# Holding back eight of the sixteen layer-2 pieces behind units 4 and 5, so that twelve are in store at each border between chunks

## The chip, the cores and the metric

The kernel runs on one core of a Trainium2 chip. The core has five engines that each take their own instructions in order: TensorE (PE in the profile; its weight loads are shown as PEld), VectorE (DVE), ScalarE (ACT), GpSimd (POOL) and SyncE (SP). SP does no arithmetic here; it only issues DMA transfers, one after the other. The metric is the time of one execution on the device in microseconds.

## The reference

Two stages follow each other. The first is a linear attention with a decaying state, for 4 batch entries, 8 heads, 768 steps and a head width of 48:

```python
for t in range(S):
    cur = np.einsum('bhd,bhe->bhde', u[None] * kt, vt)
    y[:, :, t] = np.einsum('bhd,bhde->bhe', rt, state + cur)
    state = w[None, :, :, None] * state + np.einsum('bhd,bhe->bhde', kt, vt)
```

Its output, laid out as 3072 tokens of 384 numbers, goes through a two-layer MLP with 2048 hidden units: `h = x @ w_in`, `g = h * sigmoid(h)`, `out = g @ w_out`.

## The kernel before

The 768 steps are cut into 6 chunks of 128 steps. A unit is one chunk of one batch entry, so there are 24 units, and units 4c to 4c+3 make up chunk c. For one unit the attention work is:

- `load` (line 74): three DMA transfers on SP's queue bring r, k and v.
- `turn` (line 204): TensorE transposes r and k into PSUM, and `decay` (line 210) multiplies both by their decay factors on VectorE.
- `product_pair` (line 237): for two units together, TensorE multiplies the decayed k with the decayed r. It reads the results of both `decay` calls.
- `masked` (line 244): VectorE masks the product.
- `outputs` (lines 260, 265, 275): TensorE makes the attention output (tile `yp`) and the state's increment (tile `sp`).
- `evict_y` (line 288): VectorE adds the bonus and writes `y`.
- `turn_y` (line 319): for units 6 and up a DMA transpose on SP's queue puts `y` into `xT`, the input of the MLP. For the units before, TensorE does it.
- `state` (line 299): VectorE adds the increment to the state. GpSimd makes the products with u, the decayed k and the bonus (lines 165, 167, 171, 181).

The MLP of a chunk is cut into pieces. `first(sc)` has sixteen layer-1 pieces, each of three matmuls of 128x512 (line 335) with a SiLU on ScalarE (line 338). They read `xT` of all four units of the chunk. `second(sc)` has sixteen layer-2 pieces, each of four matmuls of 128x384 (line 347); four such pieces make one block of 128 tokens, which ScalarE copies out of PSUM (line 352) and SP's queue stores (line 356).

The pieces stand in a list, `fillers`, and `fill(n)` writes the next n of them into the program at that place. If the list has run out, it writes nothing. The order of the instructions on each engine is the order in which the Python code calls them. The main loop goes over pairs of units, 4 and 5, then 6 and 7, and so on to 22 and 23. In each pass there are six places where pieces go in: four behind the product, two between the outputs of the two units, two behind the outputs, two and two around the casts of r for the next pair (`cast_r`), and four at the end. That is sixteen in one pass. With the second pair of a chunk all of `xT` has been asked for, and the chunk's 32 pieces are added to the list, just behind `outputs(i + 1)`. This place is called a border here. There are five: with units 7, 11, 15, 19 and 23.

The list begins with four layer-1 pieces and the sixteen layer-2 pieces of chunk 0. The pass of units 4 and 5 takes sixteen of these twenty. At the borders, in the kernel before, the list is empty when the 32 new pieces come.

Of the kernel before, what the change touches and what calls it, by code (L numbers as in the profile page):

```python
# [15 lines left out]
def kernel(  # L16
# [13 lines left out]
    B, H, S, D = r.shape  # L30
# [19 lines left out]
    def unit(i):  # L50
        return divmod(i, B)
# [26 lines left out]
    def load(i):  # L78
        if i >= NU:
            return  # L80
        ld(i, rin, r)
        ld(i, kin, k)
        ld(i, vin, v)
# [75 lines left out]
    def L(i):  # L159
        return live.setdefault(i, {})  # L160

    def bonus_products(i):
        n = i % NIN
        ku = wrk.tile([128, H, D], FP, name="ku")
        nc.gpsimd.tensor_tensor(out=ku, in0=kin[n][:, :, 0:D], in1=u_bc, op=ALU.mult)  # L165
        L(i)["rku_f"] = wrk.tile([128, H, D], FP, name="rku_f")
        nc.gpsimd.tensor_tensor(out=L(i)["rku_f"], in0=rin[n][:, :, 0:D], in1=ku, op=ALU.mult)  # L167

    def decayed_k(i):
        eng = nc.vector if i < B else nc.gpsimd  # L170
        eng.tensor_tensor(out=kc[i % NIN][:, :, 0:D], in0=kin[i % NIN][:, :, 0:D],  # L171
                                in1=lamC, op=ALU.mult)
# [23 lines left out]
    def turn(i):  # L196
        n = i % NIN
        t = L(i)["t"] = next_att().rearrange("p y (x g t) -> p y x g t", x=2, g=NP)
        for x, src in enumerate((rin, kin)):
            flat = src[n].rearrange("p h d -> p (h d)")  # L200
            for p in range(NP):
                for y in range(2):
                    rows = slice(HC * y, HC * y + HC)
                    nc.tensor.transpose(t[0:PR, y, x, p, :], flat[rows, 128 * p:128 * p + PR],  # L204
                                        ident[rows, rows])

    def decay(i):
        for x, key, lam in ((0, "rT", lamR), (1, "kT", lamK)):
            L(i)[key] = wrk.tile([PR, NP, C], FP, name=key)
            nc.vector.tensor_tensor(  # L210
                out=L(i)[key].rearrange("p g (y t) -> p y g t", y=2),
                in0=L(i)["t"][0:PR, :, x], in1=lam.rearrange("p g (y t) -> p y g t", y=2),
                op=ALU.mult)
# [13 lines left out]
    def product_pair(i):  # L227
        a = [next_att().rearrange("p j (g c) -> p j g c", g=NP) for _ in range(2)]
        for e in range(2):
            L(i + e)["a"] = a[e]  # L230
        for s0, c0 in ((0, 0), (HC, HC)):
            for p in range(NP):
                for e in range(2):
                    rT, kT = L(i + e)["rT"], L(i + e)["kT"]
                    o0 = s0 if e == 0 else HC - s0
                    for j, r0 in ((0, 0), (1, 64)):
                        nc.tensor.matmul(a[e][o0:o0 + HC, j, p, c0:C],  # L237
                                         kT[r0:r0 + D, p, s0:s0 + HC],
                                         rT[r0:r0 + D, p, c0:C],
                                         start=True, stop=True)  # L240

    def masked(i):
        am = L(i)["am"] = wrk.tile([128, 2, NP, C], F16, name="am")
        nc.vector.tensor_tensor(  # L244
            out=am.rearrange("p h g c -> p (h g) c"), in0=L(i)["a"].rearrange("p h g c -> p (h g) c"),
            in1=(maskX if crossed(i) else maskM).unsqueeze(1).broadcast_to([128, H, C]), op=ALU.mult)

    def outputs(i):
        sc, b = unit(i)
        v16, vy = L(i)["v16"], L(i)["vy"]  # L250
        if sc:
            yp = ps.tile([128, 512], FP, name="yp", tag="moe", bufs=4)
            L(i)["y"] = yp[:, 0:HD]
        else:
            ys = next_att()
            L(i)["y"], L(i)["sps"] = ys[:, 0, 0:HD], ys[:, 1, 0:HD]
        y = L(i)["y"].rearrange("p (h d) -> p h d", h=H)
        for p in range(NP):
            if sc:
                nc.tensor.matmul(y[:, 2 * p:2 * p + 2, :],  # L260
                                 L(i)["rT16"][0:PR, p, :],
                                 st16[b][:, p, :], start=True, stop=False)
            for j in range(2):
                h = 2 * p + j
                nc.tensor.matmul(y[:, h, :], L(i)["am"][:, j, p, :], vy[:, h, :],  # L265
                                 start=not sc, stop=(not sc or j == 1))
        if sc < NCH - 1:
            if sc:
                sp = ps.tile([128, 512], FP, name="sp", tag="moe", bufs=4)
                L(i)["sps"] = sp[:, 0:HD]  # L270
            sps = L(i)["sps"].rearrange("p (g n) -> p g n", g=NP)
            kf = kc[i % NIN].rearrange("p h d -> p (h d)")
            vf = v16.rearrange("p h d -> p (h d)")
            for p in range(NP):
                nc.tensor.matmul(sps[:, p, :], kf[:, 128 * p:128 * p + 128],
                                 vf[:, PW * p:PW * p + PW], start=True, stop=True)

    def decayed_state(i):
        sc, b = unit(i)
        if 0 < sc < NCH - 1:  # L280
            L(i)["sdec"] = wrk.tile([PR, NP, PW], FP, name="sdec")
            nc.gpsimd.tensor_tensor(out=L(i)["sdec"], in0=st[b],  # L282
                                    in1=wCT.unsqueeze(2).broadcast_to([PR, NP, PW]), op=ALU.mult)

    def evict_y(i):
        y = L(i)["y"].rearrange("p (h d) -> p h d", h=H)
        L(i)["y16"] = wrk.tile([128, H, D], F16, name="y16")
        nc.vector.tensor_tensor(out=L(i)["y16"], in0=y, in1=L(i)["vu"], op=ALU.add)  # L288

    def state(i):  # L290
        sc, b = unit(i)
        if sc == NCH - 1:
            return
        sps = L(i)["sps"].rearrange("p (g n) -> p g n", g=NP)
        for p0, c0 in ((0, 0), (64, D)):
            dst = st[b][p0:p0 + D, :, c0:c0 + D]
            src = sps[p0:p0 + D, :, c0:c0 + D]
            if sc:
                nc.vector.tensor_tensor(out=dst, in0=src,  # L299
                                        in1=L(i)["sdec"][p0:p0 + D, :, c0:c0 + D], op=ALU.add)  # L300
            else:
                nc.scalar.copy(out=st16[b][p0:p0 + D, :, c0:c0 + D], in_=src)
                nc.scalar.copy(out=dst, in_=src)
        if sc:
            nc.gpsimd.tensor_copy(out=st16[b], in_=st[b])
# [8 lines left out]
    def turn_y(i, by_pe):  # L314
        sc, b = unit(i)
        yf = L(i)["y16"].rearrange("p h d -> p (h d)")
        x = x_tile(sc)
        if not by_pe:
            nc.sync.dma_start_transpose(out=x[:, :, b, :], in_=yf)
            return  # L320
        yT = ps.tile([128, NQ, C], F16, name="yT", tag="moe", bufs=4)
        for q in range(NQ):
            nc.tensor.transpose(yT[:, q, :], yf[:, 128 * q:128 * q + 128], ident16)  # L323
        nc.scalar.copy(out=x[:, :, b, :], in_=yT)  # L324
# [35 lines left out]
    def fill(n):  # L360
        for _ in range(n):
            if fillers:
                fillers.pop(0)()

    def second(sc):
        return [lambda b=b, p=p: l2(sc, b, p) for b in range(B) for p in range(4)]

    def first(sc):
        return [lambda f=f: l1(sc, 0, B, f) for f in range(NFT)]
# [99 lines left out]
    for i in range(B, NU, 2):  # L469
        sc, b = unit(i)  # L470
        nxt = range(i + 2, min(i + 4, NU))
        product_pair(i)
        for n in nxt:
            bonus_products(n)
            decayed_k(n)
        masked(i)
        masked(i + 1)
        fill(4)
        outputs(i)
        evict_y(i)  # L480
        turn_y(i, i < 6)
        state(i)
        fill(2)
        outputs(i + 1)
        evict_y(i + 1)
        turn_y(i + 1, i < 6)
        state(i + 1)
        if b:
            fillers.extend(first(sc) + second(sc))
        fill(2)  # L490
        for n in nxt:
            turn(n)
            decay(n)
        load(i + NIN)
        load(i + 1 + NIN)
        for n in nxt:
            bonus_sum(n)
            cast_v(n)
            bonus_v(n)
            decayed_state(n)  # L500
        for n in nxt:
            fill(2)
            cast_r(n)
        fill(4)
    fill(len(fillers))


# [28 lines left out]
```

## Time and profile before

| | |
|---|---|
| median of 3 runs | 224.25 us (222.26 to 226.5) |
| the profiled execution | 223.16 us |
| its span, first to last instruction | 221.5 us |
| TensorE busy | 187.8 us, 85% of the span |
| GpSimd, ScalarE, VectorE busy | 117.4, 106.5, 101.7 us |
| mean granted clock of TensorE | 0.974 |

The profile lists, for each engine, what ran when, how long the engine had been idle ahead of it, and what ended the idle time. The granted clock is 1.00 at 2.4 GHz and 0.50 at 1.2 GHz; a value between them is a stretch that had both.

### The profile page before, as it was taken

The page shows a single profiled execution, that of the slowest core. Times are in us where ns is not written, and L with a number is a line of the kernel's source. Part 1 is how long each engine was busy: PE and PEld are TensorE (multiplying, and loading weights), DVE is VectorE, ACT ScalarE, POOL GpSimd, SP SyncE. Part 2 cuts the span into 40 slices and gives each one's busy share as a digit, 9 for nine tenths or more (in the row PEclk, how much of TensorE's full clock was granted, in tenths as well). Part 3 has the DMA queues.
Part 4 walks back from the last instruction along what each step waited for, and adds up shares of the span by engine and source line. Part 5 has one row for each costly group of instructions (what it writes and reads, how often), then busy time and mean ns, then how long its engine had stood idle before and what let it go on. Part 6 is the DMA issues. An engine that isn't in the chain of part 4 may idle for free.

```text
span 221.5 us, 5379 instructions
## 1 busy us (share of the span) xinstructions
PE 187.8 (85%) x2178; PEld 119.9 (54%) x2178; DVE 101.7 (46%) x175; ACT 106.5 (48%) x212; POOL 117.4 (53%) x151
## 2 busy tenths in 40 slices
PE   2566897989939999949999949999949999679993
PEld 1445576856715566725566615566724666424561
DVE  4675475646446266536463626464626553400021
ACT  4402758937108783019763119663129761138500
POOL 8676549995951964942956912956914902000000
PEclk9999999999996999999999988999999999979998
DMA  6899999915848017748029266019276012210011
GB/s 122 176 194 192 225 187 178 210 22 123 200 113 174 3 21 150 188 111 175 4 41 236 90 152 127 3 36 226 98 162 127 0 39 74 78 30 0 3 71 71
DMA packets 90265, 24.54 MB, mean 111 GB/s; under 512 B 83328, under 2 KB 90240, under 8 KB 90240
## 3 DMA queue, kind: packets, MB, share of 16 engines
q1 hardware_dynamic: 85824, 20.65, 42.7%
q0 software_dynamic: 3712, 3.15, 9.2%
q10 hardware_dynamic: 704, 0.40, 0.9%
q8 instruction: 17, 0.28, 0.5%
q14 instruction: 8, 0.07, 0.1%
HBM read 20.84 MB, written 4.72 MB: 115 GB/s over the span
## 4 chain that ended last, share of the span: by engine, by line
PE 72%; issue 7%; DVE 6%; DMA 5%; POOL 5%; ACT 2%; SPq 1%; ACTq 0%; POOLq 0%; DVEq 0%
PE hps L335 31%; PE ops L347 23%; PE att L237 6%; PE att L204 6%; DMA xT<-y 3%; PE att L224 2%; DMA u_bc<-in_u_dram 2%; DVE st L299 2%; DVE y L288 1%; POOL rku_f L167 1%; POOL ku L165 1%; PE yp L265 1%; PE yp L260 1%; PE yT L323 1%; ACT xT L324 1%
## 5 line engine op out<-in xcount | busy, mean ns | idle before, releaser
L335 PE MATMUL hps<-xT,win 128*128 128x512 f16 (+1 forms) x336 | 71.5, 368 | 18.0 <-DMA xT<-y 10.5
L338 ACT ACTIVATE gT<-hps 128x512 f16<-128x512 f32 x96 | 54.8, 603 | 36.2 <-PE hps L335 34.3
L347 PE MATMUL ops<-wout,gT 128*128 128x384 f16 x384 | 65.9, 326 | 0.0
L335 PEld LDWEIGHTS <-win 128*128 128x128 f16 x336 | 32.9, 103 | 47.9 <-issue 18.6
L181 POOL TENSOR_TENSOR vu<-vin,rku 128x384 f32<-128x384 f32 x24 | 19.8, 829 | 55.0 <-DVE rku L176 55.0
L347 PEld LDWEIGHTS <-gT 128*128 128x128 f16 x384 | 36.2, 98 | 23.0
L244 DVE TENSOR_TENSOR am<-att,maskM 128x1024 f16<-128x1024 f32 x14 | 17.1, 1223 | 37.9 <-PE att L237 35.4
L352 ACT COPY osb<-ops 128x384 f32<-128x384 f32 x20 | 9.6, 478 | 44.0 <-PE ops L347 44.0
L210 DVE TENSOR_TENSOR rT<-att,lamR 112x512 f32<-112x512 f32 x24 | 16.5, 686 | 30.3 <-PE att L204 15.0
L167 POOL TENSOR_TENSOR rku_f<-rin,ku 128x384 f32<-128x384 f32 x24 | 24.7, 1028 | 1.9
L165 POOL TENSOR_TENSOR ku<-kin,u_bc 128x384 f32<-128x384 f32 x24 | 24.1, 1005 | 2.8 <-DMA u_bc<-in_u_dram 1.9
L171 POOL TENSOR_TENSOR kc<-kin,lamC 128x384 f16<-128x384 f32 x20 | 20.0, 1000 | 0.0
L288 DVE TENSOR_TENSOR y<-yp,vu 128x384 f16<-128x384 f32 x20 | 11.1, 557 | 15.7 <-PE yp L265 5.1
L204 PE MATMUL att<-ident,rin 64*112 64x64 f32 x192 | 12.0, 255 | 5.8 <-DMA rin<-in_r_dram 4.0
L210 DVE TENSOR_TENSOR kT<-att,lamK 112x512 f32<-112x512 f32 x24 | 16.3, 679 | 0.0
L237 PEld LDWEIGHTS att<-rT,kT 48*64 48x64 f32 x640 | 14.3, 133 | 3.5 <-issue 3.5
L237 PE MATMUL att<-rT,kT 48*64 48x64 f32 (+1 forms) x640 | 15.7, 247 | 0.0
L204 PEld LDWEIGHTS att<-ident,rin 64*112 64x112 f32 x192 | 8.8, 155 | 11.1 <-issue 4.5
L176 DVE TENSOR_REDUCE rku<-rku_f 128x8 f32<-128x384 f32 x24 | 12.3, 541 | 4.0 <-POOL rku_f L167 4.0
L282 POOL TENSOR_TENSOR sdec<-st,wCT 112x384 f32<-112x384 f32 x16 | 13.2, 827 | 0.0
L354 DVE COPY osb<-ops 128x384 f32<-128x384 f32 x4 | 2.2, 557 | 23.7 <-PE ops L347 23.7
L244 DVE TENSOR_TENSOR am<-att,maskX 128x1024 f16<-128x1024 f32 x10 | 12.1, 1214 | 0.0
(57 smaller groups left out, 176.2 us busy)
## 6 DMA issues: line engine op xcount, KB each, us to landing
rin<-in_r_dram SPq DMA_DIRECT2D x24, 192.0 KB, 3.6
kin<-in_k_dram SPq DMA_DIRECT2D x24, 192.0 KB, 3.8
vin<-in_v_dram SPq DMA_DIRECT2D x24, 192.0 KB, 3.7
out_dram<-osb SPq DMA_DIRECT2D x24, 192.0 KB, 2.4
win<-in_moe_w_in_dram POOLq DMA_DIRECT2D x4, 384.0 KB, 6.0
wout<-in_moe_w_out_dram POOLq DMA_DIRECT2D x4, 384.0 KB, 8.2
xT<-y SPq DMA_TRANSPOSE x18, 2.3
u_bc<-in_u_dram ACTq DMA_DIRECT2D x1, 192.0 KB, 5.1
```

What stands on the lines that cost most here:

```text
L165: nc.gpsimd.tensor_tensor(out=ku, in0=kin[n][:, :, 0:D], in1=u_bc, op=ALU.mult)
L167: nc.gpsimd.tensor_tensor(out=L(i)["rku_f"], in0=rin[n][:, :, 0:D], in1=ku, op=ALU.mult)
L171: eng.tensor_tensor(out=kc[i % NIN][:, :, 0:D], in0=kin[i % NIN][:, :, 0:D], in1=lamC, op=ALU.mult)
L181: nc.gpsimd.tensor_tensor(out=L(i)["vu"], in0=vin[i % NIN], in1=L(i)["rku"].unsqueeze(2).broadcast_to([128, H, D]), op=ALU.mult)
L204: nc.tensor.transpose(t[0:PR, y, x, p, :], flat[rows, 128 * p:128 * p + PR], ident[rows, rows])
L210: nc.vector.tensor_tensor(out=L(i)[key].rearrange("p g (y t) -> p y g t", y=2), in0=L(i)["t"][0:PR, :, x], in1=lam.rearrange("p g (y t) -> ...
L237: nc.tensor.matmul(a[e][o0:o0 + HC, j, p, c0:C], kT[r0:r0 + D, p, s0:s0 + HC], rT[r0:r0 + D, p, c0:C], start=True, stop=True)
L244: nc.vector.tensor_tensor(out=am.rearrange("p h g c -> p (h g) c"), in0=L(i)["a"].rearrange("p h g c -> p (h g) c"), in1=(maskX if crossed ...
L288: nc.vector.tensor_tensor(out=L(i)["y16"], in0=y, in1=L(i)["vu"], op=ALU.add)
L335: nc.tensor.matmul(hps[:, f, :], win[:, q, (ft + f) * 128:(ft + f + 1) * 128], xts[sc][:, q, b0:b0 + nb, :].rearrange("p b t -> p (b t)"), ...
L338: nc.scalar.activation(out=gts[sc][:, ft:ft + m, b0 * C:(b0 + nb) * C], in_=hps, func=AF.Silu)
L347: nc.tensor.matmul(ops, gts[sc][:, ft, b * C:(b + 1) * C], wout[:, ft, :], start=(ft == 0), stop=(ft == NFT - 1))
```

## The change

In the pass of units 4 and 5 (`i == B`), the two `fill(2)` around `cast_r` and the `fill(4)` at the end write nothing. The eight pieces stay at the head of the list, and every later `fill` takes pieces from that list eight further back than before.

```diff
+        held = i == B
         for n in nxt:
-            fill(2)
+            fill(0 if held else 2)
             cast_r(n)
-        fill(4)
+        fill(0 if held else 4)
     fill(len(fillers))
```

At the end of the pass of units 4 and 5, TensorE's rows of the kernel before have the transposes of units 6 and 7 (L204), then 32 matmuls of layer 2 (eight pieces, each a weight load and a matmul four times), and then the product of units 6 and 7 (L237):

```order
L204 MATMUL att_70<-ident,rin_76 112x64 x8
L204 MATMUL att_70<-ident,kin_80 112x64 x8
L204 MATMUL att_69<-ident,rin_77 112x64 x8
L204 MATMUL att_69<-ident,kin_81 112x64 x8
L347 LDWEIGHTS gT
L347 MATMUL ops<-wout,gT 128x384
...
L237 MATMUL att_70<-rT,kT 64x128 x2
L237 MATMUL att_69<-rT,kT 64x128 x2
```

In the kernel after, the same place:

```order
L204 MATMUL att_70<-ident,rin_76 112x64 x8
L204 MATMUL att_70<-ident,kin_80 112x64 x8
L204 MATMUL att_69<-ident,rin_77 112x64 x8
L204 MATMUL att_69<-ident,kin_81 112x64 x8
L237 MATMUL att_70<-rT,kT 64x128 x2
L237 MATMUL att_69<-rT,kT 64x128 x2
```

The product now stands directly behind the transposes.

At the border with unit 11, TensorE's rows of the kernel before go from the last increment of the state (L275) to the first two layer-1 pieces of the new chunk (six matmuls of L335) and then to the transposes of the next pair:

```order
L275 MATMUL sp<-v_1306,kc_89 128x96
L335 LDWEIGHTS win
L335 MATMUL hps<-xT,win 128x512
...
L204 MATMUL att_70<-ident,rin_74 112x64 x8
L204 MATMUL att_70<-ident,kin_78 112x64 x8
L204 MATMUL att_69<-ident,rin_75 112x64 x8
L204 MATMUL att_69<-ident,kin_79 112x64 x8
```

In the kernel after there are eight layer-2 matmuls (two pieces) ahead of the transposes and sixteen (four pieces) behind them, and only then layer 1 of the new chunk:

```order
L275 MATMUL sp<-v_1277,kc_89 128x96
L347 LDWEIGHTS gT
L347 MATMUL ops<-wout,gT 128x384
...
L204 MATMUL att_70<-ident,rin_74 112x64 x8
L204 MATMUL att_70<-ident,kin_78 112x64 x8
L204 MATMUL att_69<-ident,rin_75 112x64 x8
L204 MATMUL att_69<-ident,kin_79 112x64 x8
L347 LDWEIGHTS gT
L347 MATMUL ops<-wout,gT 128x384
...
L335 LDWEIGHTS win
L335 MATMUL hps<-xT,win 128x512
```

So six pieces that don't read the new `xT` stand between the end of the attention and the first matmul that does. At the last border there is no next pair, and the six stand together.

On SP's queue at the same border, the kernel before has a store of a finished block between the two DMA transposes, and the loads behind them:

```order
L319 DMA_TRANSPOSE xT<-y_1443 128x3x128
L356 DMA out_dram<-osb 128x384
L319 DMA_TRANSPOSE xT<-y_1478 128x3x128
L74 DMA rin_76<-in_r_dram 128x8x48
L74 DMA kin_80<-in_k_dram 128x8x48
```

In the kernel after:

```order
L319 DMA_TRANSPOSE xT<-y_1414 128x3x128
L319 DMA_TRANSPOSE xT<-y_1447 128x3x128
L356 DMA out_dram<-osb 128x384
L74 DMA rin_76<-in_r_dram 128x8x48
L74 DMA kin_80<-in_k_dram 128x8x48
```

The store has moved behind both transposes; it is the store of a block that TensorE finishes behind the border, and the loads of units 14 and 15 stand behind it.

## Rows read from the trace of the kernel before

**Rows 1.** The page, busy time of engines; TensorE's busy tenths and clock in 40 slices.
```profile
PE 187.8 (85%) x2178; PEld 119.9 (54%) x2178; DVE 101.7 (46%) x175; ACT 106.5 (48%) x212; POOL 117.4 (53%) x151
...
PE   2566897989939999949999949999949999679993
...
PEclk9999999999996999999999988999999999979998
```

**Rows 2.** TensorE's waits: line, what it waited for, us in total, times, longest.
```profile
PE hps L335 <- DMA xT<-y: 10.5, 3, 3.8
PE hps L335 <- issue: 6.4, 2, 3.2
```

**Rows 3.** Timeline of TensorE, the borders: start, us, instruction, count, idle before and releaser.
```profile
65.29 1.67 PE L335 MATMUL hps<-xT,win 128*128 128x512 f16 x6 [3.79 <-DMA xT<-y]
...
98.60 1.46 PE L335 MATMUL hps<-xT,win 128*128 128x512 f16 x6 [3.12 <-issue]
...
130.56 2.08 PE L335 MATMUL hps<-xT,win 128*128 128x512 f16 x6 [3.33 <-DMA xT<-y]
...
163.99 1.46 PE L335 MATMUL hps<-xT,win 128*128 128x512 f16 x6 [3.25 <-issue]
...
195.32 12.22 PE L335 MATMUL hps<-xT,win 128*128 128x512 f16 x48 [3.39 <-DMA xT<-y]
```

**Rows 4.** Stretches behind borders: length, busy us of five engines, granted clock, DMA.
```profile
65.30:74.00 8.70, 8.70 (x60) 4.53 (x61) 3.40 (x6) 6.85 (x14) 2.86 (x4) 0.80 0.69 136
98.60:106.40 7.80, 7.80 (x66) 3.82 (x70) 3.40 (x6) 6.84 (x14) 2.62 (x4) 1.00 0.78 153
130.50:140.00 9.50, 9.44 (x69) 4.79 (x72) 3.40 (x6) 7.58 (x16) 3.19 (x5) 0.82 0.64 126
195.30:208.00 12.70, 12.68 (x52) 5.54 (x53) 0.00 (x0) 9.37 (x16) 0.00 (x0) 0.87 0.01 1
```

**Rows 5.** Timelines of VectorE and SP's queue at the border with unit 11.
```profile
95.40 0.56 DVE L288 TENSOR_TENSOR y<-yp,vu 128x384 f16<-128x384 f32 x1 [0.67 <-issue]
...
96.04 1.18 SPq L319 DMA_TRANSPOSE xT<-y  x1
...
102.07 0.72 SPq L74 DMA_DIRECT2D vin<-in_v_dram  x1
```

**Rows 6.** Tile xT: landing time of its DMA transposes, counted from issue.
```profile
DMA to landing us min/median/max: 2.3/2.3/3.4
```

**Rows 7.** Chain that ended last: start, us, what; pieces of both layers, transposes of a pair.
```profile
50.88 5.31 PE ops L347 x32
...
81.22 1.30 PE ops L347 x8
...
100.05 1.04 PE att L204 x32
101.09 5.29 PE hps L335 x24
```

**Rows 8.** Timelines of TensorE, VectorE, ScalarE, GpSimd behind units 4 and 5.
```profile
56.12 1.57 PE L237 MATMUL att<-rT,kT 48*64 48x128 f32 x64
...
52.35 0.68 DVE L210 TENSOR_TENSOR kT<-att,lamK 112x512 f32<-112x512 f32 x1
52.95 1.00 DVE L176 TENSOR_REDUCE rku<-rku_f 128x8 f32<-128x384 f32 x2
57.73 1.23 DVE L244 TENSOR_TENSOR am<-att,maskM 128x1024 f16<-128x1024 f32 x1 [3.79 <-PE att L237]
...
54.00 0.62 ACT L217 CAST rT<-rT 112x512 f16<-112x512 f32 x1
...
61.76 0.99 POOL L171 TENSOR_TENSOR kc<-kin,lamC 128x384 f16<-128x384 f32 x1
```

**Rows 9.** GpSimd's idle time ahead of the bonus product, two passes.
```profile
71.14 0.83 POOL L181 TENSOR_TENSOR vu<-vin,rku 128x384 f32<-128x384 f32 x1 [7.21 <-DVE rku L176]
...
118.00 0.83 POOL L181 TENSOR_TENSOR vu<-vin,rku 128x384 f32<-128x384 f32 x1 [3.28 <-DVE rku L176]
```

**Rows 10.** ScalarE behind units 12 and 13; landing of loads, tile vin from 60 us, tile rin.
```profile
112.95 0.91 ACT L190 CAST v<-vin 128x384 f16<-128x384 f32 x2
...
DMA to landing us min/median/max: 3.3/3.6/5.5
...
DMA to landing us min/median/max: 2.7/3.6/8.6
```

## The prediction

> **What bounds the kernel now.** I read the page first. TensorE is busy 85% of the span, the next engine 53%, and from about 40 us on its slices stand at nine tenths except for five dips [rows 1]. So TensorE's own time is the bound, and what can be won quickly is its idle time and its lost clock. TensorE's list of waits names the dips: 10.5 us in three waits of layer 1 (L335) for the DMA transposes into xT, and 6.4 us in two waits of the same line that carry no name but "issue" [rows 2]. The timeline then places them: 3.79, 3.12, 3.33, 3.25 and 3.39 us, each ahead of the first layer-1 matmul of a new chunk, that is, at the five borders [rows 3]. Together that is 16.88 us.
>
> The two waits called "issue" are the same wait. At the border with unit 11 VectorE's eviction ends at 95.40 + 0.56 = 95.96, the transpose is issued at 96.04 [rows 5], it lands 2.3 us later [rows 6], at 98.34, and TensorE starts at 98.60 [rows 3]. So what the border waits for is a chain of latencies (eviction, transpose, landing), not an amount of work.
>
> The third look is at the clock behind the borders. Three of the stretches have a mean granted clock below 1: 0.80 over 8.70 us, 0.82 over 9.50, 0.87 over 12.70; behind the border at 98.60 it stays at 1.00 [rows 4]. They follow the three longest gaps, 3.79, 3.33 and 3.39 us. At full clock those stretches would be 8.70 x 0.20 = 1.74, 9.50 x 0.18 = 1.71 and 12.70 x 0.13 = 1.65 us shorter. So the borders cost 16.88 of idle time and 5.10 of clock, 21.98 us.
>
> **The change, part by part.** No instruction is added or removed. Eight pieces of layer 2 leave the end of the pass of units 4 and 5, and all later pieces slide back by eight places, less the two that an empty list dropped at the border with unit 7.
>
> *The borders.* Six layer-2 pieces whose inputs are long ready now stand between the attention's last matmul and the first one that reads the new xT. Eight layer-2 matmuls (two pieces) take 1.30 us, the transposes of the next pair 1.04, and 32 of layer 2 take 5.31 [rows 7], so the four pieces behind the transposes take 2.65. The first layer-1 matmul comes 1.30 + 1.04 + 2.65 = 4.99 us after the attention, against the 3.12 to 3.79 us that it needs. Even the slowest landing, 3.4 in place of 2.3 [rows 6], leaves it covered (at most 3.79 + 1.1 = 4.89). The last border has no transposes of a next pair, and the cover is 6 x 0.66 = 3.98 against 3.39, a margin of 0.6. Here and at the borders with units 11, 15 and 19 a store no longer stands between the two DMA transposes, which can only help. I take all five gaps as gone: -16.88. With no gap ahead of them the slow stretches go too: -5.10.
>
> *The hole behind units 4 and 5.* Before, 5.31 us of pieces stand there, from 50.88 [rows 7] to 56.19. Now the product of units 6 and 7 follows directly. It reads the result of the last decay, which ends at 52.35 + 0.68 = 53.03 on VectorE [rows 8]; VectorE starts it when TensorE's transposes are done, which don't move. So the product starts at about 53.1 and TensorE idles 53.1 - 50.88 = 2.2 us. The cost lies between 0 and the whole 5.31; I take 2.2, since all else that the next steps read is there: the second cast of r ends at 54.62, the bonus sums, which stand ahead of the mask on VectorE, at 53.95 [rows 8], and the product itself would end at 54.6. The pass of 6 and 7 thus runs about 3.1 us earlier. GpSimd doesn't follow, since its work there starts with the bonus sums, which stay: it prepares units 8 and 9 until 62.75 [rows 8], and the bonus sums of that pair, the next to need it, would come at about 64.5. What is late next is nothing on TensorE's path.
>
> *What slides.* Layer-1 and layer-2 pieces take almost the same time (24 matmuls of layer 1, eight pieces, 5.29 us; eight of layer 2, 5.31 [rows 7]), so that sliding them costs TensorE nothing where their inputs are ready. In the inner passes (units 8 and 9, 12 and 13, and so on) layer 1 now ends only just ahead of the first layer-2 block of the chunk, whose fourth piece reads the last SiLUs. ScalarE is busy 6.84 of 7.80 us behind a border [rows 4] and is the tightest there. By its pace I see the SiLU done some tenths of a microsecond ahead of need. The bound is nothing or one SiLU of 0.6 us at each of four passes, 2.4 in all; I take nothing.
>
> *GpSimd and SP.* The passes get shorter by some 3 us every second pass. GpSimd waits 3.28 to 7.21 us in a pass for the bonus sums [rows 9], so it has the room. SP's loads at a border now stand behind a store that waits for two pieces (1.30) and the copy out of PSUM, and come about 0.5 us later, counted from the end of the attention. Nobody needs them for another pass: cost nothing.
>
> **The sum.** 223.16 (the profiled execution, span 221.5) - 16.88 - 5.10 + 2.2 = 203.4 us. The median of the three runs lies 1.1 above the profiled execution; I forecast 204 us, a gain of 9%.
>
> **The rivals.**
>
> *The hole is dearer.* TensorE's clock falls in the hole, or the hole is longer than 2.2. For it: the quiet stretch has transposes just ahead of it. Against it: gaps of 3.12 and 3.25 us left the clock at full [rows 3, 4]. Price: one fall, as above 1.7, gives 203.4 + 1.7 = 205.1; if the hole were also all of the 5.31, another 3.1, 208.2. The Trainium skill (TensorE: Matmul & The Clock Gate, Part 4: PE-mode transpose) states that the full clock doesn't engage for transposes on TensorE. By that rule the transposes ahead of the hole would not hold the clock up, this rival would be the case, and the sum would be 205.1 in place of 203.4; no run here shows it yet. Chance 0.11.
>
> *The two "issue" waits stay,* as they are something other than the landing. Then 6.37 us stay: 209.8. Against it stands the arithmetic of 98.34 and 98.60 above. Chance 0.04.
>
> *Small waits in the denser passes,* ScalarE's above all: 203.4 + 2.4 = 205.8, and up to 212 if the same happens at the borders. Chance 0.08.
>
> *Slower than before: SP's loads become the bound.* In an inner pass ScalarE's cast of v stands ahead of four SiLUs; if v is late, the SiLUs, the PSUM tiles and so TensorE stop. Before, the second v of such a pair is issued at 102.07 [rows 5] and read by the second cast at about 113.4 [rows 10]. After, the issue is 0.5 later and the cast 3.12 earlier, relative to the border, which leaves 7.7 us for a landing. The rows show 3.6 in the median and at most 5.5, and 8.6 for r with the crowded start included [rows 10]. Each microsecond above 7.7 costs up to one in each of four passes: at 14 us it is 4 x 6.3 = 25.2, and 228.6; the gain is eaten up from 12.7 on. Chance 0.02.
>
> *It does nothing*, since the pieces don't stand where the words say. The rows of the order show them there, so this is left with 0.01.
>
> **How the numbers follow.** The forecast has a chance of 0.74. A difference under 2% (4.5 us) can hardly be told from none here, as the three runs of before lie 1.9% apart. Below, the range reaches to a hole that costs nothing, 203.4 - 2.2 = 201.2; above, to the dearest hole with the clock and half of ScalarE's bound, 203.4 + 3.1 + 1.7 + 1.2 = 209.4, and a little further for the "issue" rival: 201 to 210. Faster by over 2% means below 219.8: forecast and the first three rivals, with little kept back for what I have not seen, 0.94; within 2% 0.03; slower 0.03.
>
> **What would show it.** In the profile after: no idle time ahead of L335 at any border; the clock at 1.00 from 40 us to the end; one new gap of about 2.2 us ahead of L237 near 51 us, released by the decay's VectorE line; TensorE's busy time 187.8 - 5.1 = 182.7 us. Wrong would be: a gap ahead of L335 that remains (the cover is too short), a gap ahead of L347 or L335 released by ScalarE in the inner passes, or GpSimd as releaser of anything on TensorE's path.

## The result, and the profile after

The changed kernel takes 202.42 us (median of 4 runs, 202.13 to 203.68) against 224.77 (222.26 to 226.5); the ratio is 0.906, with a 95% interval of 0.899 to 0.913. Two more executions of it on record, which the median leaves out, took 203.75 and 202.57 us. The forecast was 204 us, range 201 to 210.

The profiled execution took 203.68 us, its span is 202.0. On its page TensorE is busy 91% of the span in place of 85%, and the five dips are gone; one short fall of the clock is left, in the eleventh and twelfth slices [rows 1]:

```profile
PE 183.1 (91%) x2178; PEld 117.5 (58%) x2178; DVE 101.5 (50%) x175; ACT 107.8 (53%) x212; POOL 117.3 (58%) x151
...
PE   1675897996899999999999999999999999999993
...
PEclk9999999999789999999999999999999999999999
```

In the list of waits of TensorE's matmuls (line, what it waited for, us in total, times, longest) nothing waits for the DMA transposes any more [rows 2]. The new entry is the wait for the decay (L237); a wait of 0.4 us is left at one border:

```profile
PE att L237 <- DVE kT L210: 1.8, 2, 1.0
...
PE hps L335 <- DVE rku L176: 0.4, 1, 0.4
```

The timeline of TensorE from 48 us on shows all its gaps: the hole, in two parts, and 0.37 us at the border with unit 15 [rows 3, 8].

```profile
50.51 0.44 PE L237 MATMUL att<-rT,kT 48*64 48x128 f32 x4 [1.01 <-DVE kT L210]
51.71 1.55 PE L237 MATMUL att<-rT,kT 48*64 48x128 f32 x60 [0.76 <-DVE kT L210]
...
122.42 2.75 PE L335 MATMUL hps<-xT,win 128*128 128x512 f16 x12 [0.37 <-DVE rku L176]
```

The hole is in two parts because the first four matmuls of the product need the decay of unit 6 alone, and only the rest that of unit 7.

The gap of 0.37 us is named after VectorE's sums for the bonus, which end at that moment, but layer 1 does not read them. The second DMA transpose of that border was issued at 117.9 and took 4.4 us to land, so it landed at 122.3, and layer 1 started at 122.42.

In stretches (length, busy time of the five engines, granted clock, DMA), the clock falls once, behind the hole, and stays at full from 57.5 us on:

```profile
51.70:57.50 5.80, 5.79 (x77) 3.58 (x78) 3.22 (x4) 0.33 (x1) 5.23 (x7) 0.71 0.86 171
57.50:65.00 7.50, 7.50 (x98) 5.18 (x97) 5.29 (x12) 3.42 (x7) 4.68 (x6) 1.00 0.41 102
65.00:100.00 35.00, 35.00 (x457) 21.20 (x456) 18.97 (x32) 21.31 (x41) 26.34 (x32) 1.00 0.63 138
100.00:176.00 76.00, 75.63 (x961) 46.79 (x960) 40.48 (x69) 43.37 (x83) 42.70 (x51) 1.00 0.47 105
176.00:200.00 24.00, 22.46 (x123) 11.76 (x121) 2.23 (x4) 10.03 (x17) 0.00 (x0) 1.00 0.12 44
```

The fall cost 5.80 x 0.29 = 1.7 us. It came in the layer-2 matmuls that follow the product; the product's 60 matmuls took 1.55 us, as in hold8_again, where the clock did not fall. And the chain of waits (start, us, what) at the border with unit 11 is the cover itself, without a break: two pieces, the transposes of the next pair, four pieces, the new layer 1 [rows 7]:

```profile
88.53 1.30 PE ops L347 x8
89.83 1.04 PE att L204 x32
90.87 2.71 PE ops L347 x16
93.57 2.59 PE hps L335 x12
```

One more difference lies ahead of the change, where both kernels run the same instructions. The same twelve matmuls of layer 1 took 2.36 us in the execution before:

```profile
27.02 2.36 PE L335 MATMUL hps<-xT,win 128*128 128x256 f16 x12
```

and 1.48 us in the one after:

```profile
26.52 1.48 PE L335 MATMUL hps<-xT,win 128*128 128x256 f16 x12
```

By this and the rows around it, TensorE started at half its clock in both executions and reached full clock some 2.7 us earlier in the second. The transposes of unit 6 start at 48.40 there, against 49.78 (50.88 less the 1.10 of the transposes) before. This 1.4 us is the two executions' difference, not the change's.

So the two profiled executions add up: start -1.4, border gaps from 16.88 to 0.37, -16.5; clock behind the borders -5.1; hole +1.8; clock behind the hole +1.7. The sum is -19.5, and 203.68 - 223.16 = -19.48.

### The profile page after: what moved, and what is told of

Same layout as the page of the kernel before. It is cut to its first block, busy times and chain, and to the rows that moved or that the text cites. A ratio compares the mean times of both kernels' runs of the same rounds, so it can differ in the third digit from the quotient of the medians.

```text
span 202.0 us, 5380 instructions
## 1 busy us (share of the span) xinstructions
PE 183.1 (91%) x2178; PEld 117.5 (58%) x2178; DVE 101.5 (50%) x175; ACT 107.8 (53%) x212; POOL 117.3 (58%) x151
## 4 chain that ended last, share of the span: by engine, by line
PE 84%; DVE 5%; DMA 3%; ACT 2%; SPq 2%; issue 1%; DVEq 0%
PE hps L335 32%; PE ops L347 31%; PE att L237 7%; PE att L204 5%; PE att L224 3%; PE yp L265 2%; SPq L74 2%; DVE rT L210 2%; PE yp L260 2%; DMA vin<-in_v_dram 2%; DMA rin<-in_r_dram 1%; DVE kT L210 1%; PE sp L275 1%; PE yT L323 1%; ACT xT L324 1%
## 5 line engine op out<-in xcount | busy, mean ns | idle before, releaser
L335 PE MATMUL hps<-xT,win 128*128 128x512 f16 (+1 forms) x336 | 68.2, 354 | 1.5 <-ACT xT L324 1.1
L347 PE MATMUL ops<-wout,gT 128*128 128x384 f16 x384 | 68.4, 332 | 0.0
L338 ACT ACTIVATE gT<-hps 128x512 f16<-128x512 f32 x96 | 55.4, 598 | 14.1 <-PE hps L335 11.6
L347 PEld LDWEIGHTS <-gT 128*128 128x128 f16 x384 | 36.7, 99 | 24.4 <-issue 1.7
L335 PEld LDWEIGHTS <-win 128*128 128x128 f16 x336 | 31.9, 100 | 28.3 <-issue 2.1
L181 POOL TENSOR_TENSOR vu<-vin,rku 128x384 f32<-128x384 f32 x24 | 19.8, 829 | 36.9 <-DVE rku L176 33.6
L210 DVE TENSOR_TENSOR rT<-att,lamR 112x512 f32<-112x512 f32 x24 | 16.5, 687 | 14.8 <-PE att L204 6.9
L237 PE MATMUL att<-rT,kT 48*64 48x64 f32 (+1 forms) x640 | 16.1, 247 | 1.8 <-DVE kT L210 1.8
L237 PEld LDWEIGHTS att<-rT,kT 48*64 48x64 f32 x640 | 14.5, 133 | 5.3 <-issue 3.2
L204 PE MATMUL att<-ident,rin 64*112 64x64 f32 x192 | 10.7, 235 | 5.6 <-DMA rin<-in_r_dram 3.7
L204 PEld LDWEIGHTS att<-ident,rin 64*112 64x112 f32 x192 | 7.7, 139 | 10.3 <-POOL stb L128 3.7
L217 ACT CAST rT<-rT 112x512 f16<-112x512 f32 x20 | 12.4, 623 | 0.1
```

The lines of the kernel that those rows point to most:

```text
L181: nc.gpsimd.tensor_tensor(out=L(i)["vu"], in0=vin[i % NIN], in1=L(i)["rku"].unsqueeze(2).broadcast_to([128, H, D]), op=ALU.mult)
L210: nc.vector.tensor_tensor(out=L(i)[key].rearrange("p g (y t) -> p y g t", y=2), in0=L(i)["t"][0:PR, :, x], in1=lam.rearrange("p g (y t) -> ...
L237: nc.tensor.matmul(a[e][o0:o0 + HC, j, p, c0:C], kT[r0:r0 + D, p, s0:s0 + HC], rT[r0:r0 + D, p, c0:C], start=True, stop=True)
L335: nc.tensor.matmul(hps[:, f, :], win[:, q, (ft + f) * 128:(ft + f + 1) * 128], xts[sc][:, q, b0:b0 + nb, :].rearrange("p b t -> p (b t)"), ...
L338: nc.scalar.activation(out=gts[sc][:, ft:ft + m, b0 * C:(b0 + nb) * C], in_=hps, func=AF.Silu)
L347: nc.tensor.matmul(ops, gts[sc][:, ft, b * C:(b + 1) * C], wout[:, ft, :], start=(ft == 0), stop=(ft == NFT - 1))
```

## The experiments

Each is compared with the kernel before in runs on the same chip; the intervals are those of the ratio. The first three start from the kernel before or undo a part, and take the account apart into hole, clock and wait; the others change the number of held pieces and the hole. In what follows the account of the prediction is called the cover account: the border waits are the transposes' landing, six pieces cover them, and the clock was lost to the gaps. The numbers of pieces in store that the title and the expectations give (twelve; eight, ten and sixteen below) are counted at the start of a border's pass. Six of them go in ahead of the border, so that six (two, four and ten) are left at the border itself.

**hole_only: the hole without the cover.**

```diff
-        fill(4)
+        fill(12 if i == B + 2 else 4)
```

(in the changed kernel, the `fill` behind the product)

> The eight pieces are held back behind units 4 and 5, but all twelve that are then in store go in at once, behind the product of units 6 and 7, so that the list is empty at every border as in the kernel before. This leaves the hole and takes away the cover. My account: the border gaps and their slow clock stay, and the hole adds 1.8 us (as in the trace of the changed kernel) to 3.5 us (with one fall of the clock): 226.5 to 228.5 us against 224.8 before. Rival (the gain came from the order on the queues or from shorter passes, not from the cover): faster than before by 2% or more.

Measured: 227.13 us against 223.24, ratio 1.016 (1.006 to 1.026). The timeline has the hole and the border gaps of before side by side:

```profile
50.99 0.44 PE L237 MATMUL att<-rT,kT 48*64 48x128 f32 x4 [1.01 <-DVE kT L210]
52.19 1.56 PE L237 MATMUL att<-rT,kT 48*64 48x128 f32 x60 [0.76 <-DVE kT L210]
...
67.12 2.72 PE L335 MATMUL hps<-xT,win 128*128 128x512 f16 x6 [4.36 <-DMA xT<-y]
...
100.95 1.47 PE L335 MATMUL hps<-xT,win 128*128 128x512 f16 x6 [3.12 <-issue]
...
134.49 1.45 PE L335 MATMUL hps<-xT,win 128*128 128x512 f16 x6 [3.35 <-DMA xT<-y]
...
166.28 1.94 PE L335 MATMUL hps<-xT,win 128*128 128x512 f16 x6 [3.16 <-issue]
...
199.18 13.22 PE L335 MATMUL hps<-xT,win 128*128 128x512 f16 x48 [3.40 <-DMA xT<-y]
```

Holding back alone gains nothing. It costs the hole and, in this execution, more of the clock. The clock was at 1.00 in the hole, but it fell at four borders in place of three. It was 0.72 over 8.00 us behind the first gap, 0.79 over 8.00 behind the gap of 3.12 and again behind that of 3.16, and 0.81 over 12.00 in the last layer 1; behind the gap of 3.35 it stayed at 1.00:

```profile
67.00:75.00 8.00, 7.88 (x54) 4.07 (x55) 3.40 (x6) 5.49 (x11) 0.99 (x2) 0.72 0.75 148
134.50:142.00 7.50, 7.50 (x62) 3.71 (x62) 3.40 (x6) 6.55 (x14) 2.33 (x3) 1.00 0.82 159
200.00:212.00 12.00, 12.00 (x46) 4.99 (x45) 0.00 (x0) 8.56 (x15) 0.00 (x0) 0.81 0.00 0
```

The same two places, with gaps of 3.12 and 3.25 us, kept the full clock in the kernel before, and the 3.33 us before where 3.35 stand here did not [rows 3, 4].

**busy_gap: the clock without the wait.**

```diff
         if b:
+            spare = ps.tile([128, HD], FP, name="spare", tag="moe", bufs=4)
+            for m in range(20):
+                nc.tensor.matmul(spare, gts[sc - 1][:, m % NFT, 3 * C:4 * C], wout[:, m % NFT, :],
+                                 start=(m == 0), stop=(m == 19))
             fillers.extend(first(sc) + second(sc))
```

(in the kernel before)

> The kernel before, with 20 idle-time matmuls of 128x384 (3.3 us) whose result nobody reads, put at each border ahead of the first layer-1 matmul: the wait stays, but TensorE is busy in it. My account: the wait costs as much as before, the three slow stretches behind the borders go, 5.1 us less, and the longer fill adds 0.3: about 220 us. Rival (the slow clock behind a border costs nothing, since other engines set the pace there): 225 us, as before.

Measured: 218.35 us against 223.24, ratio 0.978 (0.972 to 0.984), 4.9 us less by a hundred matmuls more. TensorE's timeline at the first border shows the fill, 3.41 us, and what is left of the wait:

```profile
60.68 3.41 PE L491 MATMUL spare<-wout,gT 128*128 128x384 f16 x20
...
65.18 1.46 PE L335 MATMUL hps<-xT,win 128*128 128x512 f16 x6 [1.09 <-DMA xT<-y]
```

The six matmuls behind it take 1.46 us where they took 1.67 after the bare gap [rows 3], and the page's clock is full in all slices:

```profile
PEclk9999999999999999999999999999999999999999
```

So the slow clock behind the borders was worth about the 5.1 us that the stretches gave (the interval of the ratio allows 3.6 to 6.2), and it was due to the gaps. That the rest of the gain is the waits is shown by the next run.

**old_xT: the wait without anything else.**

```diff
-            xts[sc] = wrk.tile([128, NQ, B, C], F16, name="xT", bufs=2)
+            xts[sc] = wrk.tile([128, NQ, B, C], F16, name="xT", bufs=3)
...
-                                 xts[sc][:, q, b0:b0 + nb, :].rearrange("p b t -> p (b t)"),
+                                 xts[max(sc - 1, 0)][:, q, b0:b0 + nb, :].rearrange("p b t -> p (b t)"),
```

(in the kernel before)

> The kernel before, in which layer 1 of a chunk reads the xT of the chunk ahead of it (a third xT buffer keeps it), so that it computes layer 1 from other data and does not wait for the DMA transposes; the order of all instructions, the stores between the transposes included, is that of the kernel before, and nothing is held back. My account: all five gaps are waits for the landing, the two called issue too, and go with their slow clock: 224.8 - 16.9 - 5.1 = 202.8 us, without any hole. Rival (the two gaps called issue are something else): they stay, 6.4 us, about 209 us.

Measured: 200.54 us against 223.24, ratio 0.899 (0.893 to 0.904), 22.7 us less where the gaps and the clock make 22.0. All five gaps are gone, those called "issue" with them, and TensorE's row of the page has no dip:

```profile
PE   1566799797999999999999999999999999999992
```

The rival with the "issue" waits falls. This kernel has the stores between the DMA transposes as before, so the gain does not need the new order on SP's queue. And it is what the change could reach at best by the waits alone: the changed kernel is some 2 us above it, about the hole's 1.8.

**hold4: half the cover.**

```diff
-            fill(0 if held else 2)
+            fill(2)
```

(in the changed kernel)

> Four pieces held back in place of eight (the four of the last fill); eight are in store at a border. My account: two pieces and the transposes of the next pair, 2.3 us, stand ahead of the new layer 1 (1.3 us at the last border), so that about 5.9 us of the five gaps stay, none long enough for the clock to fall; the four pieces left behind units 4 and 5 close the hole, -1.8: 202.4 + 5.9 - 1.8 = 206.5 us. Rival (any store at a border does, whatever its size): 200.6 us.

Measured: 207.71 us against 223.24, ratio 0.928 (0.919 to 0.936). The hole is closed, and parts of the gaps are back, here in the profiled execution, the slowest of the four with 209.78 us:

```profile
63.89 5.34 PE L335 MATMUL hps<-xT,win 128*128 128x512 f16 x24 [1.72 <-DMA xT<-y]
...
93.36 5.34 PE L335 MATMUL hps<-xT,win 128*128 128x512 f16 x24 [0.95 <-DVE rT L210]
...
124.36 6.82 PE L335 MATMUL hps<-xT,win 128*128 128x512 f16 x24 [2.48 <-DMA xT<-y]
...
183.64 10.54 PE L335 MATMUL hps<-xT,win 128*128 128x512 f16 x48 [1.77 <-DMA xT<-y]
```

With 0.69 at the fourth border the gaps come to 7.6 us in this execution, more than the 5.9 worked out; and the clock was slow behind the one of 2.48 (6.82 us for 24 matmuls, against 5.34). Of the four executions two, 206.0 and 206.7 us, lie at the 206.5 that my account gave, and two lie above it; none is near the rival's 200.6.

**hold8_again, behind_turn, reordered, hold6:** these four ran side by side. hold8_again is the changed kernel itself.

> The changed kernel again, to stand beside the three variants of it in this set. My account and its rivals: 202 to 203 us, 203.7 where the clock falls in the hole.

Measured: 203.0 us (202.51 to 203.45) against 224.46, ratio 0.906 (0.902 to 0.910). Its profiled execution has the same hole, 1.01 and 0.76 us, at full clock, and no gap at any border.

behind_turn moves two pieces from ahead of the transposes of units 6 and 7 into the hole:

```diff
-        fill(2)
+        if i != B:
+            fill(2)
         for n in nxt:
             turn(n)
             decay(n)
+        if i == B:
+            fill(2)
```

> Eight held back as in the changed kernel, but in the pass of units 4 and 5 the two pieces that stood ahead of the transposes of units 6 and 7 stand behind them, in the hole. My account: the hole shrinks from 1.8 us by the two pieces' 1.3 to 0.5 and the clock cannot fall in it: 201.1 us. Rival (the hole is hidden behind GpSimd's or VectorE's work that comes later, so that filling it gains nothing): 202.4 us.

Measured: 201.44 us, ratio 0.899 (0.894 to 0.903). The hole is 0.43 us, released by the second decay, and its four first matmuls wait no longer:

```profile
51.78 1.55 PE L237 MATMUL att<-rT,kT 48*64 48x128 f32 x60 [0.43 <-DVE kT L210]
```

The gain of 1.6 us is about the hole's 1.77 less 0.43, and what the clock lost there in some executions. None of its six executions is as slow as the fastest of hold8_again. So the hole is on the path, and the rival falls.

reordered goes on in the same pass:

```diff
         evict_y(i)
+        if i == B:
+            fill(2)
         turn_y(i, i < 6)
         state(i)
-        fill(2)
+        if i != B:
+            fill(2)
         outputs(i + 1)
         evict_y(i + 1)
-        turn_y(i + 1, i < 6)
+        if i != B:
+            turn_y(i + 1, i < 6)
...
+        if i == B:
+            turn_y(i + 1, True)
+            fill(2)
```

(the `fill` of behind_turn is the last line)

> As behind_turn, and in the same pass TensorE's transposes of y wait no longer: two pieces stand ahead of the one of unit 4, and the transposes of units 6 and 7 ahead of the one of unit 5. My account: two waits of 0.5 us go; VectorE's evictions come just ahead of the decays and delay them by 0.4, so the hole is 0.9: about 200.6 us, 0.5 better than behind_turn. Rival: as behind_turn, 201.1 us, since what is won ahead of the hole makes it longer by the same.

Measured: 200.36 us, ratio 0.896 (0.891 to 0.900), the fastest kernel of this study. Its interval and that of behind_turn overlap, and the medians lie 1.1 us apart, so that it is faster than behind_turn is likely, but not shown. The two waits of 0.5 us are gone. Its only gap behind 40 us is

```profile
49.97 1.55 PE L237 MATMUL att<-rT,kT 48*64 48x128 f32 x60 [0.72 <-DVE kT L210]
```

hold6 leaves two pieces in the hole and ten in store:

```diff
-            fill(0 if held else 2)
+            fill(0 if held and n == i + 3 else 2)
```

> Six held back: two pieces stay in the hole, ten are in store at a border. My account: the hole shrinks by 1.3 to 0.5; the cover is 2.65 us of pieces and 1.04 of transposes, 3.7 against a need of 3.1 to 3.8, and 2.65 against 3.4 (less 0.4 for the store that has moved) at the last border; 0.4 to 1.5 us of gaps come back where a landing is slow: 201.5 to 202.6 us. Rival (only the full eight cover): 204 us or more.

Measured: 204.77 us, ratio 0.914 (0.909 to 0.919), 1.8 us more than with eight where my account had it equal or better. This expectation was wrong, and the rival's 204 us or more came true. The hole shrank to 0.43 as worked out, but the gaps that came back are larger, 2.8 us in all:

```profile
91.93 4.05 PE L335 MATMUL hps<-xT,win 128*128 128x512 f16 x18 [0.60 <-ACT osb L352]
...
121.82 4.04 PE L335 MATMUL hps<-xT,win 128*128 128x512 f16 x18 [1.26 <-DMA xT<-y]
...
178.04 10.53 PE L335 MATMUL hps<-xT,win 128*128 128x512 f16 x48 [0.95 <-DMA xT<-y]
```

The transpose that the gap at 121.82 waited for was issued at 117.7 and took 4.0 us to land, in place of 2.3 [rows 6]; four pieces don't cover that. The gap at 91.93 is of the same kind, though the profile names ScalarE: the second transpose of that border was issued at 88.1 and took 3.7. At the last border the landing took the usual 2.3, and four pieces without transposes are simply too few.

**hold12: more cover than needed.**

```diff
-        fill(2)
+        fill(0 if i == B else 2)
         outputs(i + 1)
...
-        fill(2)
+        fill(0 if i == B else 2)
         for n in nxt:
```

(in the changed kernel)

> Twelve pieces held back in place of eight (also the two between the outputs of units 4 and 5 and the two behind them), sixteen in store at a border, ten of them behind the attention. My account: eight already cover nearly all of the wait, at most 0.4 us of a gap is left to win in an execution, and the hole keeps its 1.8: 202 to 203 us, as with eight. Rival (each held piece is worth the same, as from four to eight): 199 us or less. Rival on the other side (less work between units 4 and 5 and the product of 6 and 7 lets GpSimd's bonus products be late there): 204 us or more.

Measured: 204.2 us (202.24 to 204.92) against 223.89, ratio 0.912 (0.907 to 0.918). No border gap is left, and nothing is won by it: eight are enough. That it is about 1 us slower than with eight, though the intervals overlap, was not in my account. The hole is the same as with eight:

```profile
48.81 0.44 PE L237 MATMUL att<-rT,kT 48*64 48x128 f32 x4 [1.01 <-DVE kT L210]
50.00 1.55 PE L237 MATMUL att<-rT,kT 48*64 48x128 f32 x60 [0.76 <-DVE kT L210]
```

but the clock falls behind it:

```profile
50.00:54.00 4.00, 4.00 (x69) 2.61 (x70) 3.22 (x4) 0.33 (x1) 4.00 (x7) 0.70 0.57 112
54.00:60.00 6.00, 6.00 (x71) 3.93 (x71) 2.35 (x6) 0.79 (x2) 5.84 (x7) 0.92 0.17 49
```

The loss is 4.00 x 0.30 + 6.00 x 0.08 = 1.7 us. Five of the six executions of hold12 have a mean clock of 0.988 to 0.992 (203.2 to 204.9 us), and the one at 1.00 took 202.2. Of the six of hold8_again, three are at 0.988 to 0.992 (203.2 to 203.5) and three at 1.00 (202.5 to 202.8). Where the clock fell is seen in the profiled execution only. The two groups of hold8_again lie 0.7 us apart and not 1.7, and one execution of the changed kernel took 203.75 at 1.00, so the clock is not all that sets executions apart. The rival with late bonus products gave the number, 204 us or more, but its mechanism does not show: no wait on TensorE names GpSimd.

## Why the prediction was right, and where its steps were off

**The borders.** Right in place and size: 16.88 us of gaps went to 0.37. That the wait is for the new xT, at all five, is shown by old_xT; and in the trace of the kernel before the first layer-1 matmul starts 0.04 to 0.2 us behind the landing of the border's second transpose, at all five. The size of the cover was nearly misjudged. The prediction took 3.4 us as the slowest landing and had 4.99 us of cover. In the profile after, the DMA transposes of xT took this from issue to landing (min, median, max):

```profile
DMA to landing us min/median/max: 2.3/2.3/4.4
```

The second transpose at the border with unit 15 took the 4.4, and there the cover ran out by 0.37. In hold8_again the same transpose took 3.9 and landed 0.1 us ahead of its matmul. With four pieces (hold6) the cover ran out at three borders. So of the step on the borders, "even the slowest landing" is what failed. It cost 0.4 us, and that it cost no more was luck: no DMA transpose in the rows of before took 4 us to land.

**The clock.** The 5.1 us are borne out by busy_gap, 4.9 measured. But the reading that the falls follow the three longest gaps is true of that one trace and does not hold as a rule. The gap of 3.12 us at the border with unit 11 left the clock at 1.00 before [rows 4], and the same 3.12 in hole_only was followed by 0.79; 3.33 was followed by a fall before, and 3.35 in hole_only was not. In the slowest execution of hold4 one of 2.48 was. So in these runs it was not the length alone that decided whether a gap costs the clock too.

**The hole.** Priced at 2.2 us, measured at 1.01 + 0.76 = 1.77, since the product starts when the first of its two units is decayed. That it is on the path is shown by behind_turn. Its rival, the clock falling there for 1.7 us more, had 0.11; in the profiled execution of the changed kernel and in that of hold12 it happened, in that of hold8_again it did not. So it is a matter of the execution, and the forecast and this rival were both true in part: by the mean clock, four of the twelve executions of the changed kernel lost some of it, so that 0.11 was low. The prediction held gaps of 3.12 and 3.25 us without a fall against it, which, as hole_only shows, was no good argument.

The Trainium skill (TensorE: Matmul & The Clock Gate, Part 4: PE-mode transpose) states that the full clock doesn't engage for transposes. That would fit a fall behind a hole of 1.8 us with transposes ahead of it, and its being more frequent in hold12 (five executions of six, against four of twelve), which has fewer matmuls ahead of them. Against it as the whole cause: in hold8_again and in hole_only the same transposes and the same hole left the clock at 1.00. No run here tried it by itself, and the cause of the fall is open.

**The slide, GpSimd and SP.** Taken at nothing, and the timeline after shows no gap on TensorE in an inner pass and none that names ScalarE or GpSimd. The rival with late loads did not come about.

**The sum.** The forecast of -19.8 us against -19.5 between the profiled executions is closer than its terms: the hole was 0.4 cheaper and the start 1.4 earlier, against a clock fall of 1.7 and 0.4 at a border. That these cancel is luck, and so is TensorE's busy time, 183.1 us against the 182.7 foretold. The profiled execution is also the only one of the four with the fall; the other three took 202.1 to 202.4 us.

## What to carry to other kernels

If an in-order engine waits at a recurring place for a chain of latencies, work it has already in store can be kept for that place. It pays once for the hole where the work is held back and gains at every later place, here 1.8 us against five times 3.4 and the clock behind them. The store has to cover the slowest landing of the new schedule, which was not the slowest of the old one; and the hole is best put where something else can slide into it.

## What the runs showed of the hardware that was not expected

- The DMA transposes of 128x384 in 16 bits landed 2.3 to 2.6 us after issue at the borders of the kernel before. In the changed kernel five of the eighteen took 3.8 to 4.4, and the same five places took 3.8 to 4.3 in the profiles of hold8_again, behind_turn and reordered, so it goes with the place in this schedule and not with the single execution. Single ones took 4.0 in hold6 and 4.1 in old_xT. old_xT has the order on SP's queue of before, so the new order alone is not what makes them slow. Nor are shorter passes alone: in busy_gap, whose passes are as long as before, those at the borders took at most 3.1, but two in the inner passes 4.5 and 4.0. What delays them is left open.
- Whether a gap on TensorE drops the granted clock was not decided by its length alone: behind 3.12 us at the same border the clock was 1.00 over 7.80 us in the kernel before and 0.79 over 8.00 in hole_only, and behind the hole of 1.01 and 0.76 us it fell in the changed kernel and in hold12, and not in hold8_again and hole_only. A drop cost 1.7 us in the changed kernel and in hold12, and 8.00 x 0.28 = 2.2 and 12.00 x 0.19 = 2.3 us at two borders of hole_only.
- TensorE ran at about half speed until 26.0 to 28.7 us in the two executions, by the durations of equal matmuls, while the granted clock of those stretches is shown as 1.00. The profile's clock there can't be relied on.
